# A recurrent attention block with a second network behind it: return transfers reordered, an inverse begun earlier in smaller portions, weight narrowing moved between engines

## The chip, the cores and the metric

The kernel runs on one core of a Trainium2 chip. The metric is the device time of one execution in microseconds (us), the median of several. Every kernel was timed in the same rounds and on the same chip as the kernel before, except the three leave-out kernels below, which ran once, with their profile; their state is unknown. The sets of rounds ran on different chips. A ratio is the mean time of one kernel's fast runs over that of the other's of the same rounds, so it is not quite the ratio of the medians quoted beside it; the bracket behind it is a 95% interval.

Engines: PE is TensorE (matmuls), PEld its weight loads, DVE is VectorE, ACT is ScalarE, POOL is GpSimd, SP is SyncE. `SPq` and `ACTq` are the DMA issues of SyncE and ScalarE.

## The reference

```python
# batch 4, 8 heads, 768 steps, head size 40; w in 0.85..0.95
for t in range(S):
    y[:, :, t] = einsum('bhd,bhde->bhe', r_t, state)
    Sa = einsum('bhde,bhe->bhd', state, a_t)
    state = state * w_t[..., None] - einsum('bhd,bhe->bhde', Sa, b_t) + einsum('bhd,bhe->bhde', v_t, k_t)
x = y as (3072, 320)
h = x @ w_in                                       # 320 x 1024
e = exp(h - max(h)); solu = h * e / (sum(e) + 1e-9)
out = ((solu - mean) / sqrt(var + 1e-6) * g_ln) @ w_out     # 1024 x 320
```

The kernel takes the 768 steps in 12 rounds of 64 steps, and each round in two "half-rounds", each with the 64 steps of 16 of the 32 pairs of batch and head: 24 half-rounds. Inside a round the dependence from step to step is a triangular system, so every round needs an inverse of 64 triangular 32x32 blocks. The weights of the second network come as float64 and are narrowed to float32 on the chip.

Of the kernel before, what the change touches and what calls it, by code (L numbers as in the profile page):

```python
# [52 lines left out]
def kernel(  # L53
# [101 lines left out]
    def narrow(dst, land, tmp):  # L155
# [9 lines left out]
        frac, rest = man.bitcast(FP32), low.bitcast(FP32)  # L165
# [3 lines left out]
        nc.scalar.activation(out=rest, in_=low.bitcast(U32), func=AF.Copy, scale=2.0 ** -52)  # L169
# [3 lines left out]
        yield  # L173
        nc.gpsimd.tensor_tensor(out=frac, in0=frac, in1=rest, op=ALU.add)
        nc.gpsimd.tensor_tensor(out=dst, in0=frac, in1=scale.bitcast(FP32), op=ALU.mult)
        yield

    def weights():
# [19 lines left out]
        if not exact:  # L198
            for tag in ("e", "lnT"):
                x = two.tile([P, 512], I64, tag=tag, name="bits", bufs=1)  # L200
                land += [x[:, 0:256], x[:, 256:512]]
            temps = [two.tile([P, 2, 256], I32, tag=tag, name="parts", bufs=1) for tag in ("osb", "parts")]
# [11 lines left out]
        for j in range(2):  # L214
            fetch(j)
        yield
        open_ = None
        for j, (dst, _) in enumerate(pieces):
            new = None if exact else narrow(dst, land[j % 4], temps[j % 2])
            for _ in range(2):  # L220
                for part in (open_, new):
                    if part:
                        next(part)
                if _:
                    fetch(j + 2)
                yield
            open_ = new
        for _ in range(2):
            if open_:
                next(open_)  # L230
# [3 lines left out]
        yield  # L234
# [3 lines left out]
        mean = bank("mean")  # L238
        for c in range(NF):
            nc.tensor.matmul(mean[:, 0:DM], lhsT=gb[:, c, :], rhs=w2[:, c, :], start=c == 0, stop=c == NF - 1)  # L240
        yield
        for c in range(NF):
            nc.vector.scalar_tensor_tensor(out=w2[:, c, :], in0=w2[:, c, :], scalar=g_col[:, c:c + 1],
                                           in1=mean[:, 0:DM], op0=ALU.mult, op1=ALU.subtract)
# [47 lines left out]
    def load(n, *names):  # L292
# [4 lines left out]
        for name in names:  # L297
# [7 lines left out]
            for c in range(2):  # L305
                nc.sync.dma_start(out=to[half(c)], in_=ap[2 * c:2 * c + 2, :, n * L:(n + 1) * L, :]
# [91 lines left out]
    def invert(n):  # L398
# [11 lines left out]
        for j in range(1, Q - 1):  # L410
# [6 lines left out]
            yield  # L417
        u_dram = of_round[n]["u"] = dram.tile([64, Q, Q], FP32, tag="u_dram", name="u_dram")
# [3 lines left out]
        for p in range(2):  # L422
            nc.sync.dma_start(out=u_dram.rearrange("b (c z) t -> b c z t", z=2)[:, :, p], in_=u[half(p)])
            if p == 0:
                nc.sync.dma_start(out=ut_dram, in_=ut)
        yield

    def bring_inverse(i):
# [5 lines left out]
        for q in (0, 2):  # L434
            for p in range(2):
                nc.sync.dma_start(out=tinv[quarter(q), :, p],
# [251 lines left out]
    def fronts(i):  # L688
# [3 lines left out]
    EARLY = ("r r a r W f r W W I r y W r W I a f a W s a f a W I W f s W I f a W L f",  # L692
             "r r a r W f g r W W I r y W r W I a f g a W s a f g a W I W f g s W I f g a W L f g")
    STEADY = "r b r a r f b b o r o I o r o y o r I o h a f L a s a h f a I h f s h f h a f h"
    front_of = {}

    front_of = {}

    front_of = {}

    front_of = {}

# [11 lines left out]
    def inverse_steps(i):  # L714

        if i < 3:
            return [[8, 8, 8, 8], [0, 3, 4, 3], [6, 6, 5, 5]][i]
        if i < LAG:
            return [0, 5, 5, 4] if i % 2 else [5, 5, 4, 4]
# [6 lines left out]
    with tc.manual_schedule():  # L726
        load(0, "w", "a", "b", "k")
        f, g = front(0), front(1)
        turns("f g", {}, f=f, g=g)
        load(1, "w", "a")  # L730
        turns("f g", {}, f=f, g=g)
        load(1, "b")
        turns("f f f f g g g g f g", {}, f=f, g=g)
        scatter(0)
        gather(0)
        load(0, "v", "r")
        load(1, "k")
        f, g, at, inv, so, ws = front(2), front(3), attend(0), invert(0), solve(0), weights()
        turns("f g f g f f g g", {}, f=f, g=g)
        load(2, "w", "a", "b", "k")  # L740
        turns("a a I a a W", dict(I=99), a=at, I=inv, W=ws)
        bring_inverse(0)
        turns("a f g a f g f g", {}, f=f, g=g, a=at)
        scatter(1)
        gather(1)
        load(1, "v", "r")
        begin(0)
        turns("s s", {}, s=so)
        inv = inverses()
        after, before = None, None  # L750
# [58 lines left out]
```

## The kernel before: what the change and the argument touch

One piece of weights is narrowed by operations spread over three engines (these are lines 162 to 175):

```python
    def narrow(dst, land, tmp):
        ...
        nc.vector.tensor_scalar(out=scale, in0=hi, ...)                  # L162
        nc.vector.tensor_scalar(out=man, in0=hi, ...)                    # L164
        yield
        nc.scalar.activation(out=scale, in_=scale, func=AF.Relu, ...)    # L167
        nc.scalar.activation(out=frac, in_=man, func=AF.Copy, ...)       # L168
        nc.scalar.activation(out=rest, in_=low.bitcast(U32), ...)        # L169
        yield
        nc.vector.scalar_tensor_tensor(out=scale, ...)                   # L171
        yield
        nc.gpsimd.tensor_tensor(out=frac, in0=frac, in1=rest, op=ALU.add)          # L174
        nc.gpsimd.tensor_tensor(out=dst, in0=frac, in1=scale..., op=ALU.mult)      # L175
        yield
```

The inverse is a chain of 30 steps on VectorE. Its blocks come through DRAM (`scatter`, then `gather` into `blk`), and its result goes back through DRAM (`u_dram`, `ut_dram`, then `tinv` and `tinvT`), because it is wanted with other rows on the partitions:

```python
    def invert(n):
        nc.vector.tensor_scalar(out=u[half(0)], in0=nb..., scalar1=-1.0, ...)      # u<-blk
        ...memsets...
        yield
        for j in range(1, Q - 1):                                                  # 30 steps
            nc.vector.tensor_tensor(out=t, in0=nb..., in1=u..., op=ALU.mult)       # prod<-blk,u
            nc.vector.tensor_tensor(out=u..., in0=u..., in1=t, op=ALU.subtract)    # u<-u,prod
            yield
        nc.vector.tensor_copy(out=ut, in_=...)                                     # ut<-u
        for p in range(2):
            nc.sync.dma_start(out=u_dram..., in_=u[half(p)])
            if p == 0:
                nc.sync.dma_start(out=ut_dram, in_=ut)
        yield
```

Every `yield` ends a portion. A string says in which order the portions of all parts are issued in a half-round, and with it the order of each engine's own instructions. `r` is the recurrence, `y` the read-out, `a` the next scores, `s` the use of the inverse (matmuls py and pz), `f` and `g` the decays of later half-rounds, `W` the narrowing, `I` the inverse:

```python
    EARLY = ("r r a r W f r W W I r y W r W I a f a W s a f a W I W f s W I f a W L f", ...)
    def inverse_steps(i):
        if i < 3:
            return [[8, 8, 8, 8], [0, 3, 4, 3], [6, 6, 5, 5]][i]
        ...
        for i in range(N):
            if i % 2 and (i + 3) // 2 < NCH:
                gather((i + 3) // 2)
            ...
            if more:
                bring_inverse(i + 1)               # tinv, tinvT on SyncE
            ...
            turns(EARLY[...] if i < LAG else STEADY, ...)        # LAG = 6
            if i % 2:
                load((i + 3) // 2, "v", "r")
                repack(i // 2)
            ...scatter
```

## Time and profile before

| | us |
|---|---|
| time, median of 3 runs | 729.5 (727.1 to 730.3) |
| first pu matmul (half-round 0 begins) | 56.6 |
| half-rounds 0 to 6, from pu to pu | 35.8, 34.0, 26.6, 31.7, 23.7, 36.3, 19.9: sum 208.0 |
| from there to the end | 463.4 |

"pu" is the first matmul of a half-round that needs the inverse, so the times between pu matmuls measure the half-rounds. From half-round 6 on the second network fills TensorE (busy 390.9 of the 405.3 us from 244.7 to 650). The granted clock in this trace is 0.5 or 1.0 in turn up to 244.9 us, 0.72 in the mean from 56.6 to 244.7, and 1.0 from there to 654.5. The views that the prediction rests on are in its text. One view that it did not use is the chain of work that ended last; this is its summary for 60 to 245 us, by line, as the answer gives it (cut at its right end):

```profile
by line: DVE prod L414 14.0%; DVE u L416 10.9%; issue 8.3%; DMA raw_b<-in_b_dram 5.7%; SPq L306 3.4%; PE mean L240 3.3%; DVE parts L162 2.9%; DVE parts L171 2.8%; PE pcx L341 2.4%; DVE parts L164 2.3%; DMA bits<-in_moe_w_out_dram 2.2%; DMA 
```

The two operations of the inverse (L414, L416) hold 24.9% of these 185 us, 46 us; VectorE's three narrowing operations (L162, L164, L171) hold another 8%.

### The profile page before, as it was taken

The page shows a single profiled execution, that of the slowest core. Times are in us where ns is not written, and L with a number is a line of the kernel's source. Part 1 is how long each engine was busy: PE and PEld are TensorE (multiplying, and loading weights), DVE is VectorE, ACT ScalarE, POOL GpSimd, SP SyncE. Part 2 cuts the span into 40 slices and gives each one's busy share as a digit, 9 for nine tenths or more (in the row PEclk, how much of TensorE's full clock was granted, in tenths as well). Part 3 has the DMA queues.
Part 4 walks back from the last instruction along what each step waited for, and adds up shares of the span by engine and source line. Part 5 has one row for each costly group of instructions (what it writes and reads, how often), then busy time and mean ns, then how long its engine had stood idle before and what let it go on. Part 6 is the DMA issues. An engine that isn't in the chain of part 4 may idle for free.

```text
span 728.0 us, 25509 instructions
## 1 busy us (share of the span) xinstructions
PE 605.3 (83%) x10873; PEld 431.6 (59%) x10873; DVE 467.5 (64%) x1258; ACT 267.2 (37%) x631; POOL 128.5 (18%) x228
## 2 busy tenths in 40 slices
PE   6436636665766899999999999999999899979997
PEld 4325525554554766677667676767677666645554
DVE  3565945855854678868868688696786763233442
ACT  4114333443441344343524443345334343322322
POOL 4104131332330111220212111220111000000000
PEclk9657576775876799999999999999999999998999
DMA  8946374455444443563555546536315231000001
GB/s 143 160 81 113 72 163 84 83 117 111 92 93 98 67 97 72 103 120 69 100 98 91 101 79 114 102 62 131 71 31 104 53 60 34 21 24 18 19 5 32
DMA packets 269793, 59.84 MB, mean 82 GB/s; under 512 B 255464, under 2 KB 265328, under 8 KB 269680
## 3 DMA queue, kind: packets, MB, share of 16 engines
q1 hardware_dynamic: 265680, 52.73, 39.8%
q10 hardware_dynamic: 4000, 5.48, 2.9%
q8 instruction: 86, 1.41, 0.8%
q14 instruction: 27, 0.22, 0.1%
HBM read 40.08 MB, written 13.37 MB: 73 GB/s over the span
## 4 chain that ended last, share of the span: by engine, by line
PE 58%; DVE 22%; DMA 7%; issue 5%; ACT 4%; SPq 3%; POOL 1%; ACTq 0%; DVEq 0%; POOLq 0%
PE po L662 14%; PE h L617 12%; DVE prod L414 7%; DVE u L416 6%; PE pyo L589 4%; PE plnT L657 3%; PE pcx L341 2%; PE pcum L328 2%; DVE nmax L627 2%; PE plamv L280 2%; PE py L484 2%; DMA raw_b<-in_b_dram 2%; PE pyo L511 2%; PE pvT L261 2%; PE ppsi L280 1%
## 5 line engine op out<-in xcount | busy, mean ns | idle before, releaser
L617 PE MATMUL h<-w_in,xT 128*128 128x512 f32 (+1 forms) x288 | 128.2, 635 | 3.9 <-DVE e L634 3.9
L662 PE MATMUL po<-w,lnT 128*128 128x320 f32 x384 | 114.8, 438 | 0.0
L414 DVE TENSOR_TENSOR prod<-blk,u 128x30 f32<-128x30 f32 (+4 forms) x360 | 107.0, 297 | 11.8 <-DMA blk<-blk_dram 1.0
L416 DVE TENSOR_TENSOR u<-u,prod 128x30 f32<-128x30 f32 (+4 forms) x360 | 101.5, 282 | 12.4
L662 PEld LDWEIGHTS po<-w,lnT 128*128 128x128 f32 x384 | 68.8, 190 | 26.2 <-issue 2.9
L331 POOL TENSOR_TENSOR kx<-raw_b,inv 128x320 f32<-128x320 f32 x24 | 20.7, 866 | 254.8 <-ACT inv L329 210.1
L627 DVE TENSOR_REDUCE nmax<-h 128x1 f32<-128x1024 f32 x24 | 29.3, 1221 | 44.8 <-PE h L617 44.8
L617 PEld LDWEIGHTS h<-w_in,xT 128*128 128x128 f32 (+1 forms) x288 | 38.2, 191 | 31.6 <-issue 29.7
L484 PE MATMUL py<-tinv,nt 32*32 32x32 f32 x768 | 20.6, 202 | 34.2 <-DMA tinv<-ut_dram 34.2
L667 ACT ACTIVATE osb<-po,rs 128x320 f32<-128x320 f32 x24 | 12.7, 527 | 97.2 <-PE po L662 86.4
L596 DVE TENSOR_TENSOR x<-pyo,kx 128x512 f32<-128x512 f32 x24 | 16.6, 690 | 45.2 <-PE pyo L589 44.5
L282 DVE TENSOR_TENSOR lamv<-plamv,cst 128x512 f32<-128x512 f32 x24 | 16.5, 689 | 39.8 <-PE plamv L280 39.8
L649 POOL TENSOR_TENSOR rs<-c,mhalf 128x1 f32<-128x1 f32 x24 | 13.2, 548 | 158.4 <-DVE c L648 158.4
L658 ACT COPY lnT<-plnT 128x512 f32<-128x512 f32 x48 | 27.6, 586 | 33.8 <-PE plnT L657 33.5
L631 ACT ACTIVATE e<-h,nmax 128x1024 f32<-128x1024 f32 x24 | 26.7, 1114 | 36.1 <-DVE nmax L627 36.1
L484 PEld LDWEIGHTS py<-tinv,nt 32*32 32x32 f32 x768 | 17.2, 112 | 36.7 <-issue 29.3
L634 DVE TENSOR_TENSOR e<-h,e 128x1024 f32<-128x1024 f32 x24 | 29.4, 1225 | 14.6 <-ACT e L631 14.2
L499 ACT ACTIVATE tinvT<-pz 32x256 f32<-32x256 f32 x48 | 17.9, 372 | 56.9 <-PE pz L484 56.6
L341 PEld LDWEIGHTS pcx<-cst,lw 128*128 128x128 f32 x192 | 29.1, 209 | 14.9 <-ACT y_mid L496 8.5
L341 PE MATMUL pcx<-cst,lw 128*128 128x132 f32 x192 | 33.6, 307 | 5.3 <-ACT y_mid L496 3.4
L657 PE MATMUL plnT<-cst,e 128*128 128x128 f32 x192 | 29.9, 285 | 5.7 <-DVE e L634 5.4
L575 POOL TENSOR_TENSOR sm<-tot,fac 128x320 f32<-128x320 f32 x20 | 14.8, 742 | 95.2 <-DVE tot L574 79.2
(104 smaller groups left out, 1121.3 us busy)
## 6 DMA issues: line engine op xcount, KB each, us to landing
blk<-blk_dram SPq DMA_DIRECT2D x24, 256.0 KB
raw_w<-in_w_dram SPq DMA_DIRECT2D x24, 160.0 KB
raw_a<-in_a_dram SPq DMA_DIRECT2D x24, 160.0 KB
raw_b<-in_b_dram SPq DMA_DIRECT2D x24, 160.0 KB
raw_k<-in_k_dram SPq DMA_DIRECT2D x24, 160.0 KB
v<-in_v_dram SPq DMA_DIRECT2D x24, 160.0 KB
r<-in_r_dram SPq DMA_DIRECT2D x24, 160.0 KB
out_dram<-osb SPq DMA_DIRECT2D x24, 160.0 KB
```

The lines of the kernel that those rows point to most:

```text
L341: nc.tensor.matmul(t[:, g * 132:g * 132 + 132], lhsT=pair(lw, 2 * j + g), rhs=cst[:, lo:lo + 132], start=True, stop=True)
L414: nc.vector.tensor_tensor(out=t, in0=nb[:, j:j + 1, j + 1:Q].to_broadcast([P, rows, m]), in1=u[:, 0:rows, j:j + 1].to_broadcast([P, rows, ...
L416: nc.vector.tensor_tensor(out=u[:, 0:rows, j + 1:Q], in0=u[:, 0:rows, j + 1:Q], in1=t, op=ALU.subtract)
L484: nc.tensor.matmul(t[quarter(out), c:c + Q], lhsT=lhs(p, g), rhs=rhs(p, g), start=True, stop=True)
L589: nc.tensor.matmul(t[half(p), c, g * W:g * W + used], lhsT=kb[half(c), j, 2 * g + p, :], rhs=lam[half(c), h % 2, h // 2, 0:used], start=i ...
L617: nc.tensor.matmul(h[:, j * 512:j * 512 + 512], lhsT=of_round[i // 2]["xT"][rows, kt, i % 2 * P:i % 2 * P + P], rhs=w_in[rows, 4 if kt == ...
L627: nc.vector.tensor_reduce(out=nmax, in_=h, axis=AX.X, op=ALU.max, negate=True)
L631: nc.scalar.activation(out=e, in_=h, func=AF.Exp, bias=nmax, accum_out=esum)
L634: nc.vector.tensor_tensor(out=q, in0=h, in1=e, op=ALU.mult)
L657: nc.tensor.transpose(out=t[:, j * P:(j + 1) * P], in_=q[:, f * P:(f + 1) * P], identity=ident)
L658: nc.scalar.copy(out=lnT[:, fs.start:fs.stop].rearrange("p f t -> p (f t)"), in_=t)
L662: nc.tensor.matmul(o[:, 0:DM], lhsT=lnT[:, f, :], rhs=w2[:, f, :], start=f == 0, stop=f == NF - 1)
```

## The change

Its intent: TensorE waited for inverted blocks that were issued behind bulk loads, so issue them first; begin the second inverse while the first one's result travels; cut the inverse into small portions so that nothing waits long behind it; take the narrowing's last two operations off GpSimd, beside which VectorE's operations took longer (an inverse step's product of 126 columns 0.85 us at 79.99, with GpSimd's narrowing running, and 0.29 us at 75.07, with GpSimd idle); and do the centring of `w2` in half-rounds 6 and 7, not in a burst before them. The diff, cut to its core:

```diff
@@ narrow
-        nc.scalar.activation(out=rest, in_=low.bitcast(U32), func=AF.Copy, scale=2.0 ** -52)
-        nc.gpsimd.tensor_tensor(out=frac, in0=frac, in1=rest, op=ALU.add)
-        nc.gpsimd.tensor_tensor(out=dst, in0=frac, in1=scale.bitcast(FP32), op=ALU.mult)
+        nc.vector.scalar_tensor_tensor(out=frac, in0=low.bitcast(U32), scalar=2.0 ** -52, in1=frac, ...)
+        nc.vector.tensor_tensor(out=dst, in0=frac, in1=scale.bitcast(FP32), op=ALU.mult)
@@ weights: three pieces fetched ahead instead of two; four sets of temporaries instead of two;
@@          the centring becomes a part of its own, centre()
@@ invert
+        other = nc.scalar if n == 0 else nc.sync
-                nc.sync.dma_start(out=ut_dram, in_=ut)
+                other.dma_start(out=ut_dram, in_=ut)
@@ bring_inverse: for i == 0, half of tinv is issued by ScalarE
@@ order of portions
-    EARLY = ("r r a r W f r W W I r y W r W I a f a W s a f a W I W f s W I f a W L f", ...
+    EARLY = ("r r a I r f r W r I W y I r W W a f L a I W s W a f a W I f s W I f a W I W f", ...
-        if i < 3:
-            return [[8, 8, 8, 8], [0, 3, 4, 3], [6, 6, 5, 5]][i]
+        if i == 0:
+            return [3, 3, 3, 3, 3, 3, 2]
         if i < LAG:
-            return [0, 5, 5, 4] if i % 2 else [5, 5, 4, 4]
+            return [0, 0, 2, 4, 4, 4, 3 if i < LAG - 1 else 0] if i % 2 else [3, 3, 3, 3, 3, 0, 0]
@@ start
-        load(0, "w", "a", "b", "k")
+        load(0, "w", by=(nc.sync, nc.scalar)); load(0, "a"); load(0, "b", by=act); load(0, "k")
+        load(0, "v", "r", by=act)                   # act: both halves issued by ScalarE
...
         scatter(0)
+        load(1, "k")
         gather(0)
+        load(2, "w", "a"); load(1, "v", "r")
-        turns("a a I a a W", dict(I=99), a=at, I=inv, W=ws)
-        bring_inverse(0)
+        turns("a f g W a a W f f W a g g W a", {}, f=f, g=g, a=at, W=ws)
+        turns("I f g f g I f g", dict(I=[8, 8]), f=f, g=g, I=inv)
+        scatter(1); load(2, "b", "k"); gather(1)
+        turns("I a", dict(I=99), a=at, I=inv)
+        bring_inverse(0)
...
+        turns("I s s", dict(I=12), s=so, I=inv)     # 12 portions of the second inverse
@@ main loop
+            if more and (i % 2 or i == 0):
+                bring_inverse(i + 1)                # ahead of the gather
             if i % 2 and (i + 3) // 2 < NCH:
                 gather((i + 3) // 2)
-                bring_inverse(i + 1)
...
             if i % 2:
+                if i + 2 < N:
+                    bring_inverse(i + 2)            # ahead of v, r, the repacking and the scatter
                 load((i + 3) // 2, "v", "r")
```

## The prediction

> **What bounds the kernel now.** I read the page first (clock and busy rows), then the busy table cut at four points, then the waits of one stage, then SyncE's, TensorE's and VectorE's instructions in order of time. A half-round is one value of the loop's index i; I mark it by the start of its matmul group pu: 56.6, 92.4, 126.5, 153.1, 184.8, 208.5, 244.7 and 264.6 us for i = 0 to 7. From i = 6 on, the second network's h and po matmuls fill TensorE.
>
> The busy table (columns: stretch, length, busy us of PE, PEld, DVE, ACT, POOL, granted clock, DMA share, GB/s) cut there:
>
> ```profile
> 0.00:56.60 56.60, 27.36 (x376) 21.37 (x376) 29.31 (x89) 14.43 (x31) 13.58 (x31) 0.73 0.77 127
> 56.60:244.70 188.10, 117.99 (x2500) 96.19 (x2499) 122.41 (x358) 71.22 (x191) 53.83 (x88) 0.72 0.52 100
> 244.70:650.00 405.30, 390.94 (x7757) 274.80 (x7757) 285.78 (x755) 161.85 (x374) 57.29 (x102) 1.00 0.42 79
> 650.00:728.00 78.00, 68.99 (x243) 39.22 (x241) 29.96 (x56) 19.72 (x35) 3.84 (x7) 0.94 0.08 20
> ```
>
> From 244.7 us TensorE is busy 96% of the time at full clock; that part cannot move much. Before it nothing is full: TensorE 63%, VectorE 65%, clock 0.72. So the gain has to come out of the first 245 us, where chains of waits rule. The waits of 56 to 245 us (total, times, longest):
>
> ```profile
> PE py L484 <- DMA tinv<-ut_dram: 32.5, 8, 12.8
> POOL w_in L175 <- DVE parts L171: 28.5, 5, 10.1
> DVE u L404 <- DMA blk<-blk_dram: 8.9, 3, 5.4
> DVE parts L162 <- POOL w_in L175: 7.6, 2, 7.0
> DVE parts L162 <- POOL w L175: 5.3, 2, 4.9
> ```
>
> TensorE waits 32.5 us for inverted blocks. VectorE waits 12.9 us for GpSimd's narrowing. Why the blocks are late shows on SyncE's queue:
>
> ```profile
> 93.07 2.38 SPq L306 DMA_DIRECT2D raw_b<-in_b_dram  x2
> 95.55 3.62 SPq L306 DMA_DIRECT2D raw_k<-in_k_dram  x2
> 99.26 2.74 SPq L389 DMA_DIRECT2D blk_dram<-nt  x4
> 103.49 1.12 SPq L396 DMA_DIRECT2D blk<-blk_dram  x2
> 109.32 1.79 SPq L436 DMA_DIRECT2D tinv<-ut_dram  x4
> ```
>
> ```profile
> 91.14 0.63 DVE L420 COPY ut<-u 128x512 f32<-128x512 f32 x1
> ```
>
> ```profile
> 111.89 0.28 PE L484 MATMUL py<-tinv,nt 32*32 32x32 f32 x2 [12.80 <-DMA tinv<-ut_dram]
> ```
>
> The second inverse is finished at 91.1 us, but its way back (tinv) is issued only at 109.3, behind b, k, the scatter and the next gather; TensorE idles 12.8 us.
>
> [...]VectorE in order of time, one step with GpSimd's narrowing beside it and the next without:
>
> ```profile
> 79.99 0.85 DVE L414 TENSOR_TENSOR prod<-blk,u 128x126 f32<-128x126 f32 x1
> 80.87 0.29 DVE L416 TENSOR_TENSOR u<-u,prod 128x126 f32<-128x126 f32 x1
> ```
>
> [...]the DMA engines' busy share is already 0.85 to 1.17 from 2 to 16 us. [...]
>
> **The change part by part.**
>
> *Narrowing.* 26 pieces (10 of 256 columns, 16 of 160) lose two GpSimd operations and one ScalarE operation each, and gain two on VectorE. [...]the existing scalar_tensor_tensor (L171, same sizes) starts its successor after 0.33 or 0.24. So VectorE gains 10 x 0.66 + 16 x 0.48 = 14.3 us. It gets back contention: the 60 big instructions of an inverse take 16.4 us busy between 220 and 262 us (no narrowing) but 18.8, 19.7 and 19.1 in the three before, 8.4 us together, and the 12.9 us waits on GpSimd go. So about neutral in VectorE's time, better in coupling.
>
> *Inverted blocks first.* From i = 1 the order on SyncE is u, ut, u, scatter, tinv and tinvT, then gather, then the odd half's blocks, v, r, xT. Way back instead of 18 us from the end of the inverse to the issue: u's issues 2, scatter 3, landing about 4.5 in parallel, tinv issue, landing: first py about 9.5 us after ut, as in the undisturbed first inverse (44.5 us end, 52.6 most of py). That removes the 12.8 and the 8.7 us waits of i = 1 and i = 3, and most of those of even i.
>
> *First inverse.* Against it: v, r and three weight pieces (0.65 and 0.79 MB) are now issued before the first scatter. At the 165 GB/s seen there this is over 8 us of transfers in a stretch that is already full, of which I put 7 ahead of or beside scatter and gather; ScalarE spends about 3.4 us issuing loads in the front chain, inside this. The first inverse (24.2 us now) starts near 31, carries two kx and two nt (2.7 us) inside, loses some contention, ends near 53.5. Its return with two issuing queues takes about 11 us to pu instead of 12: first pu near 64.6, **8 us later** than now. In that return VectorE starts the second inverse (u must first be read out, some 4 us; then 1.4 + 11 steps at 0.5), so 14 of its 31 portions are done when lamu of i = 0 comes.
>
> *Half-rounds.* VectorE's work in one, read from distances of starts: half an inverse 9.5 (30 steps 17.1, set-up 1.4, ut 0.6), five narrowed pieces at 1.4 or 1.0, masks and sums 6 x 0.6 + 2 x 0.4 = 4.4. TensorE's: about 13.5 us at full clock, up to 20 at half.
> - 0 to 1: pu to lamu 4.5, then 17 steps 9.7, five pieces 7, other 4.0, ut and nt 1.2, hand-over 1: 27 (now 35.8).
> - 1 to 2: 2.2 + 9.8 + 6.6 + 4.4 + 1 = 24 on VectorE; TensorE: py 8.2 after pu, then 14.6 as now, 23. So 24 (now 34.1).
> - 2 to 3, 3 to 4, 4 to 5: 2 + 9.5 + 5.1 + 4.4 + 1.5, so 22.5, 23, 22 (now 26.6, 31.7, 23.7).
> - 5 to 6: the centring (mean: 3.9 us wait and 6.1 us at half clock) is gone from here, narrowing too; TensorE sets it: 20 (now 36.2).
> - 6 to 7: 19.9 plus the mean matmuls at full clock, 3.1, and about 1 of waiting for gb: 24 (now 19.9).
>
> Sum 162.5 against 208.0: 45.5 saved, minus 8 at the start: **37.5**. After i = 7 nothing changes, since TensorE is the bound there and its work is the same. 729.5 - 37.5 = **692 us**.
>
> **Rivals.**
> *VectorE becomes the bound of the early stage and takes the gain.* For it: by my sums it is 85 to 90% full in i = 1 to 4, [...]and ScalarE's narrowing waits for it (43.7 us of such waits now), so a late VectorE delays copies that TensorE needs. If each of i = 1 to 4 costs 4 us more: 708. Against: the inverse comes in portions of two to four steps, so chain work waits at most about 2 us.
> *The early loads cost more than they give.* [...]the first scatter may stand behind all the weight bytes. Start 15 us later rather than 8: 699. If instead the small transfers slip through, 4 us: 688.
> *The clock helps more than I count.* If the early stage runs at full clock, the TensorE-led pieces of i = 1 to 5 shrink by 2 to 3 us each: about 680. [...]
> *The gain is hidden*, the second network's work catching up at the end. Against: from 244.7 us on TensorE has no idle time to absorb it, so an earlier begin of i = 6 is an earlier end.
>
> **Range and chances.** The rivals give 680 to 708; the sum has seven terms of 1.5 to 4 us error each and a start of 4: 677 to 709 should hold it 8 times in 10. Slower than 715 needs the first two rivals together and more: faster by over 2% 0.92, within 2% 0.07, slower 0.01.
>
> **What would show it.** First u step near 31 us, first pu near 64.6; second inverse's ut near 90; pu of i = 6 near 203 and of i = 7 near 227, and equal distances from there to the end. PE py waits on tinv after 70 us under 8 us in total. Inverse instructions near 17 us each with no 0.7 us ones beside narrowing. VectorE over 80% busy from 65 to 183 us. The prediction is wrong if the first pu comes after 72 us, if the half-rounds of i = 1 to 4 stay above 26 us, or if a new wait (TensorE for ScalarE copies behind narrowing) exceeds 15 us.

## The result, and the profile after

The changed kernel takes **737.7 us** (735.0 to 740.7, 4 runs) against 728.7 (727.1 to 730.3, 4 runs) for the kernel before in the same rounds: ratio 1.012 [1.008, 1.017]. It is not faster, it is 1% slower. Behind the narrowing and its helpers, line numbers of the changed kernel are 5 to 6 higher than before. The profiled run of the changed kernel took 740.7 us, the slowest of its four; that of the kernel before took 729.8 us.

| us | before | predicted | after |
|---|---|---|---|
| first inverse starts | 24.2 | 31 | 35.1 |
| first pu | 56.6 | 64.6 | 70.3 |
| half-round 0 | 35.8 | 27 | 30.5 |
| 1 | 34.0 | 24 | 34.5 |
| 2 | 26.6 | 22.5 | 26.8 |
| 3 | 31.7 | 23 | 33.7 |
| 4 | 23.7 | 22 | 26.4 |
| 5 | 36.3 | 20 | 24.2 |
| 6 | 19.9 | 24 | 26.7 |
| sum of these | 208.0 | 162.5 | 202.8 |
| from there to the end | 463.4 | unchanged | 465.8 |

Predicted were +8 at the start and -45.5 in the half-rounds; the profiled run has +13.7, -5.2, and +2.4 in the rest, together +10.9. So two terms failed: the half-rounds by 40 us, the start by 6.

The busy table of the changed kernel, cut at its own first pu and sixth half-round (columns as in the prediction):

```profile
0.00:70.30 70.30, 24.47 (x378) 19.55 (x378) 33.45 (x113) 15.68 (x35) 13.47 (x31) 0.74 0.78 131
70.30:246.40 176.10, 116.98 (x2483) 96.39 (x2482) 119.13 (x379) 61.43 (x159) 22.27 (x36) 0.69 0.47 94
```

VectorE is busy 119 of 176 us, 68% against 65% before: still not full. The granted clock was 0.69, against 0.72. The waits of 70 to 246 us (total, times, longest):

```profile
ACT parts L167 <- DVE parts L162: 51.5, 15, 11.2
PE py L490 <- ACT vT L268: 20.1, 3, 10.5
DVE u L409 <- DMA blk<-blk_dram: 16.3, 3, 6.1
PE py L490 <- DMA v<-in_v_dram: 10.4, 1, 10.4
```

TensorE's wait for tinv, 32.5 us before, is gone. In its place py waits 30.5 us for something else: 20.1 for ScalarE's copy vT and 10.4 put down to v. What that is shows in half-round 1. First SyncE, then VectorE, ScalarE and TensorE of the changed kernel in order of time:

```profile
104.84 3.21 SPq L442 DMA_DIRECT2D tinv<-ut_dram  x4
108.15 1.89 SPq L445 DMA_DIRECT2D tinvT<-u_dram  x4
110.08 1.13 SPq L401 DMA_DIRECT2D blk<-blk_dram  x2
```

```profile
106.95 0.68 DVE L602 TENSOR_TENSOR x<-pyo,kx 128x512 f32<-128x512 f32 x1
113.72 0.42 DVE L409 TENSOR_SCALAR u<-blk 64x512 f32<-64x512 f32 x1 [6.10 <-DMA blk<-blk_dram]
...
117.05 0.28 DVE L162 TENSOR_SCALAR parts<-bits 128x256 int32<-128x256 int32 x1
```

```profile
117.37 0.51 ACT L167 ACTIVATE parts<-parts,ebias 128x256 int32<-128x256 int32 x1 [9.70 <-DVE parts L162]
117.58 0.35 ACTq L211 DMA_DIRECT2D bits<-in_moe_w_out_dram  x1
117.79 0.40 ACT L168 ACTIVATE parts<-parts 128x256 f32<-128x256 int32 x1
118.09 0.56 ACT L268 COPY vT<-pvT 128x512 f32<-128x512 f32 x1
```

```profile
118.71 1.13 PE L490 MATMUL py<-tinv,nt 32*32 32x32 f32 x32 [10.37 <-DMA v<-in_v_dram]
```

Read from the bottom: py begins at 118.71. tinv was issued at 104.84, so it is not the cause any more. py starts 0.06 us after the end of the copy vT (118.09, 0.56 us long). py does not use vT; but the program gives py the PSUM bank that the copy reads out, and the waits above hold 20.1 us of py for this copy. vT stands in ScalarE's order behind the narrowing L167, which waited 9.70 us for VectorE's L162. L162 stands in VectorE's order behind the head of the next inverse, `u<-blk`, and that waited 6.10 us for `blk`, whose gather is now issued behind tinv and tinvT. VectorE, ScalarE and TensorE stand in a convoy, one behind the other, and at its head is one transfer. The waits stand behind one another in the order in which the program issues the portions: 6.10 us on VectorE, 9.70 on ScalarE and 10.37 on TensorE.

At the start, ScalarE's first issues and its first activation:

```profile
4.91 3.50 ACTq L311 DMA_DIRECT2D v<-in_v_dram  x2
8.46 3.98 ACTq L311 DMA_DIRECT2D r<-in_r_dram  x2
12.49 0.83 ACT L329 ACTIVATE lw<-raw_w 128x320 f32<-128x320 f32 x2 [10.47 <-DMA raw_k<-in_k_dram]
```

Before, this activation began at 5.86. ScalarE is held 7.5 us issuing v and r (four issues of 1.05 to 2.12 us, and 1.2 us of wait between two of them), and its first arithmetic stands behind that.

### The profile page after: what moved, and what is told of

It is laid out like the page before. It is cut to its first block, busy times and chain, and to the rows that moved or that the text cites.

```text
span 738.9 us, 25449 instructions
## 1 busy us (share of the span) xinstructions
PE 609.6 (83%) x10873; PEld 436.0 (59%) x10873; DVE 471.5 (64%) x1310; ACT 260.4 (35%) x606; POOL 97.7 (13%) x176
## 4 chain that ended last, share of the span: by engine, by line
PE 59%; DVE 23%; DMA 6%; ACT 5%; issue 4%; SPq 2%; ACTq 1%; DVEq 0%
PE po L668 14%; PE h L623 12%; DVE prod L419 6%; DVE u L421 6%; PE pyo L595 4%; PE plnT L663 3%; DMA blk<-blk_dram 3%; PE pcum L333 2%; PE plamv L285 2%; PE pcx L346 2%; DVE nmax L633 2%; PE pyo L517 2%; PE py L490 2%; PE plamu L285 2%; ACT e L637 1%
## 5 line engine op out<-in xcount | busy, mean ns | idle before, releaser
L421 DVE TENSOR_TENSOR u<-u,prod 128x30 f32<-128x30 f32 (+4 forms) x360 | 97.8, 272 | 12.4
L419 DVE TENSOR_TENSOR prod<-blk,u 128x30 f32<-128x30 f32 (+4 forms) x360 | 96.3, 267 | 10.5
L336 POOL TENSOR_TENSOR kx<-raw_b,inv 128x320 f32<-128x320 f32 x24 | 20.8, 866 | 312.1 <-ACT inv L334 287.0
L490 PE MATMUL py<-tinv,nt 32*32 32x32 f32 x768 | 19.9, 204 | 47.8 <-ACT vT L268 20.1
L633 DVE TENSOR_REDUCE nmax<-h 128x1 f32<-128x1024 f32 x24 | 29.3, 1220 | 43.5 <-PE h L623 43.5
L623 PEld LDWEIGHTS h<-w_in,xT 128*128 128x128 f32 (+1 forms) x288 | 37.7, 189 | 30.9 <-issue 28.9
L602 DVE TENSOR_TENSOR x<-pyo,kx 128x512 f32<-128x512 f32 x24 | 16.6, 690 | 50.4 <-PE pyo L595 50.0
L505 ACT ACTIVATE tinvT<-pz 32x256 f32<-32x256 f32 x48 | 17.9, 373 | 64.3 <-PE pz L490 61.7
L637 ACT ACTIVATE e<-h,nmax 128x1024 f32<-128x1024 f32 x24 | 26.7, 1114 | 36.7 <-DVE nmax L633 36.7
L640 DVE TENSOR_TENSOR e<-h,e 128x1024 f32<-128x1024 f32 x24 | 29.4, 1224 | 14.4 <-ACT e L637 13.9
L346 PE MATMUL pcx<-cst,lw 128*128 128x132 f32 x192 | 33.2, 302 | 6.3 <-ACT rT L268 3.9
L287 DVE TENSOR_TENSOR lamv<-plamv,cst 128x512 f32<-128x512 f32 x24 | 16.6, 690 | 30.3 <-PE plamv L285 30.3
L333 PE MATMUL pcum<-lw,cst 128*128 128x320 f32 x48 | 22.7, 564 | 15.3 <-ACT lw L329 13.5
L663 PE MATMUL plnT<-cst,e 128*128 128x128 f32 x192 | 30.5, 289 | 5.6 <-DVE e L640 5.3
```

The costliest lines, as they stand in the source:

```text
L333: nc.tensor.matmul(t[:, 0:DM], lhsT=c_("cum_in"), rhs=lw[:, :, 0:D], start=True, stop=True)
L346: nc.tensor.matmul(t[:, g * 132:g * 132 + 132], lhsT=pair(lw, 2 * j + g), rhs=cst[:, lo:lo + 132], start=True, stop=True)
L419: nc.vector.tensor_tensor(out=t, in0=nb[:, j:j + 1, j + 1:Q].to_broadcast([P, rows, m]), in1=u[:, 0:rows, j:j + 1].to_broadcast([P, rows, ...
L421: nc.vector.tensor_tensor(out=u[:, 0:rows, j + 1:Q], in0=u[:, 0:rows, j + 1:Q], in1=t, op=ALU.subtract)
L490: nc.tensor.matmul(t[quarter(out), c:c + Q], lhsT=lhs(p, g), rhs=rhs(p, g), start=True, stop=True)
L623: nc.tensor.matmul(h[:, j * 512:j * 512 + 512], lhsT=of_round[i // 2]["xT"][rows, kt, i % 2 * P:i % 2 * P + P], rhs=w_in[rows, 4 if kt == ...
```

## The experiments

Seventeen kernels besides the changed one ran on the chip. Their diffs are cut to the core, that of the lag is condensed; marks like `...` stand for what is left out. "Gather first", below, is the changed kernel with one exchange (the second experiment), and later experiments build on it. All results agree with the reference, except where said.

| kernel | median us (range) | ratio to before |
|---|---|---|
| changed kernel | 737.7 (735.0–740.7) | 1.012 [1.008, 1.017] |
| changed, first loads from SyncE | 737.6 (733.9–741.1) | 1.011 [1.007, 1.015] |
| changed, gather first | 723.5 (721.6–724.6) | 0.991 [0.989, 0.994] |
| changed, inverse begun late | 725.5 (724.4–726.4) | 0.994 [0.992, 0.996] |
| changed, narrowing back on GpSimd | 729.4 (728.2–732.2) | 1.001 [0.998, 1.004] |
| gather first and late | 729.4 (725.9–732.8) | 0.997 [0.993, 1.001] |
| changed, all first loads from SyncE | 734.5 (732.1–734.8) | 1.003 [1.001, 1.006] |
| changed, gather behind first return | 736.9 (735.2–738.3) | 1.007 [1.004, 1.010] |
| before, late centring alone | 728.9 (726.3–730.3) | 0.996 [0.993, 0.999] |
| gather first, old start | 725.2 (723.3–726.9) | 0.993 [0.989, 0.997] |
| gather first, no inverse steps | 691.4 (one run) | |
| gather first, no narrowing | 700.6 (one run) | |
| gather first, lag | 719.2 (717.0–723.4) | 0.986 [0.982, 0.990] |
| gather first, old start, return from SyncE | 722.1 (718.8–724.0) | 0.988 [0.984, 0.992] |
| the same, lag | **717.5** (716.2–718.3) | **0.982** [0.979, 0.986] |
| before, inverted blocks first alone | 729.8 (728.8–730.3) | 0.999 [0.996, 1.002] |
| before, no inverse steps | 684.4 (one run) | |
| the 717.5 version, weights behind the return | 723.8 (722.2–726.5) | 0.992 [0.990, 0.994] |

The kernel before was at 729.5 to 731.2 us in these rounds.

### Is the convoy the cause? Gather first; inverse late

Two ways to keep VectorE from standing at the head of the next inverse. One puts the gather back ahead of the inverted blocks:

```diff
-            if more and (i % 2 or i == 0):
-                bring_inverse(i + 1)
             if i % 2 and (i + 3) // 2 < NCH:
                 gather((i + 3) // 2)
+            if more and (i % 2 or i == 0):
+                bring_inverse(i + 1)
```

> The changed kernel with the order of before on SyncE: the gather of the next round's blocks ahead of the inverted blocks of this one. Theory C (in the changed kernel VectorE stands 6.1 us at i = 1 and 3 before the first portion of the next inverse, waiting for its gather, and the narrowing's ScalarE part and the copies behind it stand too, so py waits 10 us): VectorE's waits for blk shrink under 2 us each, py waits for tinv itself again, half-rounds 1 and 3 change by less than 3 us in sum, total within 4 us of 738. Rival O (inverted blocks first is a pure gain that other parts of the change hide): half-rounds 1 and 3 longer by 6 us or more each, total 748 or more. Rival O' (the new order is the harm): total 728 or less.

The other leaves the order of transfers and begins the next inverse later in odd half-rounds:

```diff
-            return [0, 0, 2, 4, 4, 4, 3 if i < LAG - 1 else 0] if i % 2 else [...]
+            return [0, 0, 0, 0, 5, 6, 6 if i < LAG - 1 else 3] if i % 2 else [...]
```

> The changed kernel with the portions of the inverse in odd half-rounds moved behind py: 0 0 0 0 5 6 6 instead of 0 0 2 4 4 4 3, so that no inverse step that needs the gathered blocks stands in VectorE's order before the work that py waits for. Theory C (VectorE stands in order before the gathered blocks and takes ScalarE and TensorE with it): VectorE's waits for blk in half-rounds 1, 3 and 5 under 1 us, the wait before py in half-round 1 down from 10.4 to about 3 us, half-rounds 1, 3 and 5 shorter by 4 to 6 us each at first and up to 2 given back where the portions are now larger: total 725 to 730. Theory V (VectorE is simply full with the narrowing it took over): VectorE's idle time moves but half-rounds stay within 1.5 us, total within 3 us of 738.

Measured: 723.5 and 725.5, so each takes back what the change lost, and they are 6.5 and 4.4 us below the kernel before of these rounds. The late inverse came out in the range that theory C gave. The gather first did not: theory C had expected a total within 4 us of 738 and half-rounds 1 and 3 shorter by less than 3 us in sum (6.0 measured); the total is that of rival O', that the new order is the harm. SyncE shows why: the gather came 3.7 us earlier (106.38 instead of 110.08 us) and tinv only 2.8 us later (107.61 instead of 104.84), so both were early enough. Its waits, to be set beside those of the changed kernel (16.3 us for blk; 30.5 us of py for vT and v):

```profile
PE py L490 <- ACT vT L268: 25.0, 4, 8.1
...
DVE u L409 <- DMA blk<-blk_dram: 5.3, 2, 3.2
```

So the convoy is real, and on SyncE the changed order does harm; but most of py's wait stays when blk comes in time, and what holds vT then is examined below. The half-rounds 1 to 5 became 31.3, 24.7, 30.9, 25.6, 21.1 with the gather first, and 29.8, 27.0, 29.6, 26.0, 20.8 with the late inverse. They did not fall to the predicted 20 to 24. TensorE's waits with the late inverse, 71 to 245 us:

```profile
PE py L490 <- ACT vT L268: 15.3, 4, 5.3
PE pu L556 <- DVE x L537: 14.5, 3, 5.3
```

VectorE no longer waits for blk, but now pu waits 14.5 us for VectorE's sum x, which stands behind the portions of the inverse that were moved later. The wait moved once more.

Both at once:

> The changed kernel with both cures of the convoy at once: the gather of the next inverse ahead of the inverted blocks on SyncE, and the next inverse begun late in odd half-rounds. Theory C (one convoy: VectorE stands at the head of the next inverse, whose blocks have not landed, and ScalarE's narrowing and copies and TensorE stand behind it): both cure the same wait, so the two do not add: 719 to 724 us against 723.5 and 725.5 apart. Rival, two separate costs (blocks late; VectorE full early in the half-round): they add, about 711 us.

It gave 729.4, worse than either. Half-rounds 1 and 3 are 31.3 and 29.7, no better than with one of them, so these two cure one wait and do not add, as the theory said; but half-round 5 lengthened to 24.2 and the later half-rounds by 2 us, which neither expectation has (both gave less than 725), and which was not followed up. (Its profile is of a run of 731.6 us, 2 us above its median.)

### Narrowing back on GpSimd

```diff
-        nc.vector.scalar_tensor_tensor(out=frac, in0=low.bitcast(U32), scalar=2.0 ** -52, in1=frac, ...)
-        nc.vector.tensor_tensor(out=dst, in0=frac, in1=scale.bitcast(FP32), op=ALU.mult)
+        nc.gpsimd.tensor_tensor(out=frac, in0=frac, in1=rest, op=ALU.add)
+        nc.gpsimd.tensor_tensor(out=dst, in0=frac, in1=scale.bitcast(FP32), op=ALU.mult)
```

(and ScalarE's operation for `rest` back)

> The changed kernel with the narrowing's addition and product back on GpSimd (and the third ScalarE operation), all else as changed. Theory V (the 14 us that VectorE took over are what ate the gain): half-rounds 1 to 4 shorter by about 2.5 us each, total 727 to 730. Theory C: the stand before blk is the same, contention with GpSimd comes back (about 2.5 us an inverse), half-rounds unchanged or longer: total 737 to 744.

729.4, 8 us below the changed kernel: the total that theory V gave. Half-rounds 1 to 4 (33.2, 25.2, 33.1, 25.1) fell by only 1.2 us each on average, not 2.5, and VectorE's wait for blk stayed (16.0 us). So taking the narrowing off GpSimd removes contention (the inverse's two operations sum to 194.1 us in the changed kernel, against 208.5 before and 205.2 here), but costs more than it gives back. That the cost lies in VectorE's order is argued, not shown. The narrowing on GpSimd together with the gather first was not run.

### What VectorE's work costs: leave it out

These three tell the most. First the 30 steps of every inverse after the first are left out, on "gather first"; set-up, read-out and all transfers stay. This is not the reference's arithmetic and no version to keep, although its result still passed the comparison.

```diff
         for j in range(1, Q - 1):
+            if n > 0:
+                yield
+                continue
```

> The version with the gather first, but of every inverse after the first only the set-up, the read-out and the transfers are left: its 30 steps on VectorE are gone, so the result is wrong on purpose. Theory V (TensorE waits in the early half-rounds because its scores, sums and copies stand in VectorE's order behind portions of the inverse, directly and through ScalarE): half-rounds 1 to 4 fall from 31.3, 24.7, 30.9, 25.6 us to 21 to 24 each, and the waits of py and pu fall under 8 us together. Rival (a chain through TensorE and ScalarE sets the half-round whatever VectorE does): they stay above 25 us on average.

Then the narrowing, its seven operations replaced by one copy on GpSimd (wrong result):

> The version with the gather first, with the narrowing's five VectorE and two ScalarE operations a piece replaced by one copy on GpSimd: wrong result on purpose, same transfers. Theory V expects half of what leaving out the inverse gives, since it is 5 to 7 us of VectorE in a half-round against 9: half-rounds 1 to 4 shorter by 3 us each on average, py waiting for the copy vT under 8 us in all instead of 25. Rival (only the inverse's portions block, the narrowing slips into gaps): under 1 us each.

And the first cut on the kernel before:

> The kernel before without the 30 steps of each inverse after the first (its set-up, read-out and transfers stay; not the reference's arithmetic). Theory V (VectorE's time for the inverse is paid in full in the early stage, before and after the change): about 30 us below the kernel before, near 698, as in the changed order (32 below). Rival (before, TensorE waited for transfers, so VectorE's time was hidden there, and the change only exposed it): less than 15 us below.

| four half-rounds, 1 to 4 | time us | VectorE busy us | TensorE busy us | granted clock |
|---|---|---|---|---|
| before | 116.0 | 76.8 | 71.2 | 0.72 |
| before, no inverse steps | 93.5 | 41.4 | 64.3 | 0.80 |
| gather first | 112.5 | 78.4 | 74.5 | 0.70 |
| gather first, no inverse steps | 97.0 | 50.4 | 67.6 | 0.77 |
| gather first, no narrowing | 98.5 | 54.1 | 72.1 | 0.76 |

The first two rows are read from these lines:

```profile
92.42:208.45 116.03, 71.17 (x1656) 59.03 (x1656) 76.83 (x224) 47.63 (x133) 37.44 (x63) 0.72 0.52 102
83.09:176.63 93.54, 64.33 (x1658) 53.38 (x1657) 41.37 (x105) 47.26 (x133) 36.97 (x60) 0.80 0.63 128
```

A microsecond of VectorE's work left out takes 0.63 us off the time in the kernel before (22.5 for 35.4), 0.56 and 0.58 with the gather first. These figures hold more than VectorE's order: the granted clock rose too, by 0.06 to 0.08, and TensorE's busy time fell by 2.3 to 6.9 us for the same matmuls; and without the narrowing ScalarE's work fell as well (41.9 to 29.8 us). How much of the gain each of these gives was not separated. Half-rounds 1 to 4 of "gather first" become 26.1, 22.3, 23.9, 24.6 without the inverse: the first and the last of them missed the expected 21 to 24, and py still waited 16.7 us for vT, so the waits did not fall under 8 as theory V expected; the times fell all the same. Without the narrowing, py's wait for vT fell to 9.8 (under 8 expected), and the four half-rounds became 3.5 us shorter on average (3 expected).

On the kernel before, the run without the inverse is the sharpest. Its waits between 56 and 245 us:

```profile
PE py L487 <- DMA tinv<-ut_dram: 30.6, 8, 12.6
```

TensorE still waits 30.6 us for tinv, nearly as much as before (32.5), with nearly the same longest wait. Yet the kernel takes 684.4 us, 45 less than the 729.5 on the same chip, where theory V expected 30. About 37 of the 45 us are won before half-round 7 begins (at 227.7 instead of 264.6 us), the rest behind it. The chain that ended last, by engine, in the kernel before and in this one:

```profile
PE 58%; DVE 22%; DMA 7%; issue 5%; ACT 4%; SPq 3%; POOL 1%; ACTq 0%; DVEq 0%; POOLq 0%
```

```profile
PE 72%; DMA 9%; DVE 7%; SPq 4%; ACT 3%; issue 3%; POOL 1%; DVEq 0%; POOLq 0%; ACTq 0%
```

VectorE falls from 22% of 728 us (160) to 7% of 683 (48); most of that share goes to TensorE, so the chain's share is not the time to be won. But in the early half-rounds of both orders more than half of the inverse's time on VectorE is paid for, although VectorE is busy only 65% of the time, and this gain does not need the wait to go that the change set out to remove.

### Inverted blocks first, alone, on the kernel before

```diff
+            if more and (i % 2 or i == 0):
+                bring_inverse(i + 1)
             if i % 2 and (i + 3) // 2 < NCH:
                 gather((i + 3) // 2)
...
-                bring_inverse(i + 1)
...
             if i % 2:
+                if i + 2 < N:
+                    bring_inverse(i + 2)
                 load((i + 3) // 2, "v", "r")
```

> The kernel before with one part of the change alone: inverted blocks issued ahead of the gather, and the odd half-round's ahead of v, r, the repacking and the scatter. The prediction's step: the waits of py for tinv, 32.5 us in all, nearly go and about 20 us of time with them: 710. Rival (the wait is exchanged: the next inverse's blocks come later, VectorE stands at their head, and ScalarE's narrowing and TensorE behind it): waits of py for tinv under 10 us, VectorE's for blk up by more than 10, and the total within 5 us of the kernel before.

729.8 against 729.5: nothing, with 0.999 [0.996, 1.002]. Its waits of 56 to 245 us, to be set beside those that the prediction shows:

```profile
DVE u L404 <- DMA blk<-blk_dram: 24.9, 3, 8.7
...
PE py L484 <- DMA tinv<-ut_dram: 9.6, 4, 5.2
```

py's wait for tinv falls by 22.9 us (32.5 to 9.6), VectorE's for blk rises by 16.0 (8.9 to 24.9), and the half-rounds (33.8, 27.3, 32.6, 24.8 for 1 to 4) are those of before within 1.2 us. py also gets waits for ScalarE that it did not have before, 5.8 us for vT and 4.6 for an operation of the narrowing. The rival holds in all its numbers. This step by itself is worth zero, because the wait is exchanged; the prediction had counted most on it. What the wait would be worth if nothing else came later, no run shows.

### ScalarE's part one portion later ("lag")

```diff
             for turn in range(2):
-                if open_ and turn == 0:
-                    next(open_)
-                if new:
+                if new and turn == 0:
                     next(new)
+                if open_:
+                    next(open_)
                 if turn:
                     fetch(j + 3)
                 yield
             open_ = new
```

> The version with the gather first, with ScalarE's part of every narrowed piece issued one portion later, so that VectorE's first part lies further back. Theory (ScalarE stands behind a VectorE operation that itself stands behind the inverse, and the copy vT behind ScalarE): py's waits for vT fall from 25 to under 12 us, total 2 to 6 us below 723.5. Rival (the later portion also stands behind a portion of the inverse; the wait only moves): within 2 us of 723.5.

719.2: 4 us below "gather first", in the expected range; py's waits for vT fell to 12.2 us, just over the expected 12 (in a profiled run of 723.4 us, the slowest of the four). ScalarE's wait for L162 (43.5 us with the gather first) fell to 3.1, with 8.9 for another of VectorE's narrowing operations: so what coupled the two engines was in good part that ScalarE was given work that VectorE had not yet come to.

### The start

Five kernels, because each showed another cause.

*First loads as before, v and r behind the first gather.*

```diff
-        load(0, "w", by=(nc.sync, nc.scalar)) ... load(0, "v", "r", by=act)
+        load(0, "w", "a", "b", "k")
...
         gather(0)
+        load(0, "v", "r")
```

> The changed kernel with the first loads as before: all of w, a, b, k from SyncE, and v and r of round 0 from SyncE behind the first gather; the weight pieces stay early on ScalarE. Theory S (ScalarE is held by issuing v and r [...]3.5 and 4.0 us in the trace of the changed kernel, so its first Ln starts at 12.5 instead of 5.9 us): first Ln near 6 us, first step of the first inverse near 28 instead of 35 us, first pu near 64 instead of 70.3, total 6 to 7 us faster than the changed kernel, 731. Rival (the early transfers as such fill the DMA engines, whoever issues them; v and r only come later now and the weights still stand before the scatter): first inverse no earlier than 33 us, total within 2 us of 738.

737.6, no gain. The first activation is back at 5.8 us, but the first inverse starts at 38.1: the changed order puts the scores that need v and r ahead of the inverse on VectorE, and with v and r late they hold it (the copy vT of these scores runs at 31.53 us, in the changed kernel at 25.9). The rival's numbers came true (no earlier than 33 us, total within 2 us of 738), but the run mixed two things up and decides nothing.

*All first loads from SyncE, v and r with them:* `load(0, "w", "a", "b", "k", "v", "r")`.

> The changed kernel with every first load, v and r among them, on SyncE in the order w, a, b, k, v, r. Theory S (ScalarE's first activations are late only because it was held while issuing v and r; the first inverse is late because of that): the first decay starts near 6 us instead of 12.5, the first inverse near 29 instead of 35.1, the first pu near 65 instead of 70.3, total 5 to 6 us below the changed kernel, about 732. Rival (the first inverse is late because the forward steps of the first scores are put ahead of it on VectorE, whatever the loads): the first inverse stays above 33 us and the total above 735.

734.5: first activation at 5.9, but the first inverse at 33.8, not 29, and the first pu at 68.9, 1.4 us earlier. At the first pu ScalarE's hold is worth 1.4 us; the rest is neither theory's:

```profile
20.89 3.46 SPq L394 DMA_DIRECT2D blk_dram<-nt  x4
24.45 1.78 SPq L311 DMA_DIRECT2D raw_k<-in_k_dram  x2
30.26 1.12 SPq L401 DMA_DIRECT2D blk<-blk_dram  x2
```

The blocks were written by VectorE at 18.8 us, scattered from 20.9, and gathered only at 30.3, 9.4 us after the scatter's issue; before it was 4.4 (16.30 to 20.71 us). Between them stands the load of k that the change puts there (1.78 us), and SyncE waits for weight pieces to land, 2.6 us at the gather. The prediction's rival "the early loads cost more than they give" is this.

*Gather of the second inverse behind the first one's return* (one line, `gather(1)`, moved behind `bring_inverse(0)`).

> The changed kernel with the gather for the second inverse issued behind the first inverse's return instead of ahead of it. Theory (that gather waits on SyncE for the read-out of ut, and u's read-out stands behind it): the way from the end of the first inverse to the first pu falls from 14.4 to about 11.5 us, but the second inverse's blocks land later; total 1 to 3 us below the changed kernel. Rival (the return is bound by the transfers themselves): the first pu is within 1 us of 70.3 and the total is the same.

First pu 67.6, 2.7 us earlier, as the theory said; but the second inverse waits 11.9 us for its blocks, half-round 0 grows from 30.5 to 34.2, and the total is 736.9. The 95% interval of the ratio (1.004 to 1.010) overlaps that of the changed kernel. A gain at one place, given back at the next.

*The old start,* on "gather first": loads and order from before up to the first pu, and `[5, 5, 5, 5, 4, 4, 4]` portions of the second inverse in half-round 0. Two things stay as changed: half of the return is issued by ScalarE, and four more portions of the narrowing stand beside it.

> The version with the gather first (723.5 us) and, besides, the kernel before's order from the first load to the first pu: no weights, v or r ahead of the first scatter, the first inverse ahead of the forward steps of the scores, the second inverse begun only in half-round 0. Theory (the new start costs 14 us at the first pu and gives back 5 in half-round 0): first pu near 57 us, half-round 0 near 35, all later half-rounds as with the gather first, total near 714. Rival (the second inverse, not begun early, and the narrowed pieces, fewer by then, come due later and take it back): the later half-rounds grow and the total is 720 or more.

725.2, a total in the rival's range, but not for the rival's reason. The first inverse starts at 25.0 and ends at 44.8 as before, but the first pu comes at 64.5. SyncE's longest wait between 28 and 60 us:

```profile
SPq L311 <- DMA ut_dram<-ut: 13.9, 1, 13.9
```

L311 is a load of b for a later round. It shares no data with ut. What the traces of the kernel before and of the changed one show of this: the 646 issues of both queues carry eight semaphore numbers between them, 80 or 81 issues to each. In all 638 pairs of successive issues with one number, the landing records of the first end before the second is issued; in 17 of these pairs before and 28 in the changed kernel the second follows the last record within 0.2 us (there SyncE's blk, which shares no data with ut either, waited 5.7 us and was issued at 58.66 us, 0.06 us after ScalarE's ut had landed). In the run here the second half of b, on SyncE, was held in the same way until ScalarE's ut had landed: the first half was issued at 32.63 us, the second at 47.46. u, tinv and tinvT stood behind it. With these transfers on SyncE again:

```diff
-        other = nc.scalar if n == 0 else nc.sync
+        other = nc.sync
...
-                (nc.scalar if i == 0 and q else nc.sync).dma_start(out=tinv[...
+                nc.sync.dma_start(out=tinv[...
```

> The last version with the kernel before's start (gather first besides), and now the first inverse's way back issued wholly from SyncE, as before, instead of half from ScalarE. Theory (in the run with the old start the first pu came at 64.5 instead of 57 us because a load of b on SyncE stood 13.9 us for ScalarE's ut transfer, with which it shares no data, and u, tinv and tinvT behind it): that wait is gone, first pu near 57.5, total 717 to 721. Rival (the narrowing put beside the return costs the 7 us): first pu stays above 62 and the total at 725.

722.1, the first pu at 61.2: half of the expected way. The wait of 13.9 us is gone, but another of 9.6 us, for a weight piece, stands in its place. With the lag besides:

> The same, with ScalarE's part of each narrowed piece one portion later: all that helped so far in one kernel. If the gains add (start 5, lag 4 on 723.5), about 714, 2.2% below the kernel before. Rival (they relieve the same wait): 718 or more.

**717.5 us**, 1.8% below the kernel before and 2.7% below the changed one (737.7, in other rounds), the best of all. Of the steps from "gather first" (0.991) to here only the whole is clear of noise; the intervals of neighbouring steps overlap. The gains add only in part: first pu 61.6, half-rounds 36.2, 30.2, 25.4, 30.5, 24.2, 19.7, 25.4. Its longest wait on SyncE between 40 and 60 us is, again, one on weights:

```profile
SPq L446 <- DMA bits<-in_moe_w_in_dram: 7.6, 2, 7.4
```

So the last kernel fetches the first weights only behind the first inverse's return:

> The best version so far with the first weight pieces fetched and narrowed only behind the first inverse's way back. In its trace tinv's issue stood 7.4 us for the landing of a weight piece. Theory: that wait is gone, the first pu near 57 instead of 61.6 us, and 3 to 5 us of it stay in the total: 713 to 715. Rival (the pieces, five portions later, come due in the early half-rounds or in a burst before half-round 6): total within 1.5 us of 717.5.

A miss: 723.8, first pu 63.0. Now the return's second transfer, ut, waited 5.5 us for g_rows, a small load of the second network. The source has g_rows behind the return, and ScalarE issued it only at 49.32 us, 4.6 us after the first part of u (44.72); yet ut, issued at 50.81, stood behind its landing. In this run who waited for whom followed neither the source nor the time. The kernel before's own arrangement, one portion of weights ahead of the return and none beside it (first pu 56.6), was not run with the gather first.

### The late centring alone

The kernel before with `centre()` as in the change, from half-round 6 on.

> The kernel before with the late centring alone. If the traces' gaps are to be added (36.3 to 24.2 us in one half-round, 19.9 to 26.7 in the next), it is 5 us faster, about 724. Rival (the next half-round gives it all back): within 2 us of the kernel before.

728.9 against 731.2: 0.996 [0.993, 0.999], some 3 us. It lies between the expected 5 and the rival's 2. The gain of half-round 5 (36.3 to 28.2) is partly given back in 6 (19.9 to 25.4).

## Why the prediction was wrong

**The bound.** Right: nothing is full in the early stage, chains rule it, and after half-round 7 nothing changes (465.8 against 463.4 us). Wrong: "chains of waits" were sized by the waits' totals. TensorE's 32.5 us for tinv were taken for time to be won. The runs show otherwise from both sides: taking 22.9 us of this wait away changed nothing, since other waits came in its place, and taking VectorE's steps away while 30.6 us of it remained gave 45 us. The chain of work that ended last pointed at the inverse (46 us of it in 60 to 245 us; that the two numbers are so close is chance). The prediction did not use it.

**Inverted blocks first.** The mechanism of the way back was right: tinv is issued 5.9 us after ut in the changed kernel (98.9 to 104.8), 18.2 before, and the wait for it is gone. (The 9.5 us from ut to py that the prediction reads from the first inverse are 8.1 in the times it names, 44.5 to 52.6; nothing hangs on this.) The failed step is "That removes the 12.8 and the 8.7 us waits of i = 1 and i = 3": it was checked what the moved transfers overtake, but not what then waits for the overtaken ones. The overtaken gather stands at the head of VectorE's next inverse.

**The half-rounds**, 162.5 predicted, 202.8 measured. This is the term that was wrong by 40 us. Most of them were worked out as VectorE's work laid end to end plus about 1 us. The work itself was sized rightly: in half-rounds 1 to 4 VectorE was busy 78.5 us, 86% of the predicted 91.5, as "85 to 90% full" has it. The step that failed is the end to end: these half-rounds took 121.4 us, and VectorE was idle in 43 of them. From 65 to 183 us it was busy 69%, where the prediction named over 80% as its sign (68% before). It does not get its work end to end: it takes turns with TensorE and ScalarE in a fixed order, and leaving work out between the turns shortened them by 0.56 to 0.63 us for each us, the faster clock included. (Without the inverse's steps the seven half-rounds of "gather first" come to 162.8 us. That this is the predicted sum is chance: the prediction counts about 9.5 us of the inverse in most of them.)

**"The inverse comes in portions of two to four steps, so chain work waits at most about 2 us."** This set aside the rival that came true in part, that VectorE takes the gain: VectorE was not full, but ScalarE's narrowing waited for it, as the rival says (51.5 us, 43.7 before). A portion's length bounds the wait only if the portion can run when it is reached. The first one could not (6.1 us for blk in half-round 1), and the wait went on to ScalarE (9.70) and TensorE (10.37). Two of the three signs of failure that the prediction named came: half-rounds 1 to 4 above 26 us (34.5, 26.8, 33.7, 26.4), and TensorE behind ScalarE's copies behind the narrowing for over 15 us (30.5). The third, a first pu after 72 us, did not (70.3).

**Narrowing, "about neutral in VectorE's time, better in coupling".** The first half was right: VectorE's busy time over the whole kernel went from 467.5 to 471.5 us, and the contention that the move removes was seen rightly (the inverse's two operations 194.1 us instead of 208.5). The second was not: in the changed order the move costs 8 us (737.7 against 729.4 with the operations back on GpSimd).

**The first inverse**, "8 us later": 13.7. Its own length was right (20.8 us with the added work inside; 22.5 predicted). Too small were the loads ahead of it (start at 35.1, not 31), where ScalarE's hold (6.6 us at the first activation, 1.4 of it in the time) and the gather behind bulk and weights (9.4 us instead of 4.4 in the run that separates them) come together, and the return, 14.4 us instead of the predicted 11.

**The centring.** Half-round 5 gave 12.1 us of the predicted 16; half-round 6 took 6.8 and not 4. Its mean matmuls, 6.1 us before, ran at a granted clock of 0.5 up to 221.0 us, half of that time, and at 1.0 from there; in the changed kernel, at 1.0, they took 4.6 us, not 3.1. Alone it is worth 3 us. The mechanism was right; the sizes of what is won and given back were not.

**The rest.** The 2 to 3 us that the rival "the clock helps more than I count" has for each of i = 1 to 5 at full clock are the author's estimate; the clock came out lower (0.69 against 0.72). What stays open: what moves the granted clock between 0.5 and 1.0, which no run shows; how much of what the leave-out runs gave is VectorE's order and how much the clock; whether the narrowing on GpSimd adds to the gather first; why "gather first" and "late inverse" together are slower than either, and what holds the first pu at 61.6 us in the best version beyond the wait for weights.

## What to carry to other kernels

A wait in the profile is worth its length only if what it waits for can come earlier without something else coming later, and if the waiting engine's chain is the one that ends last; so read the chain of work first, and leave the suspected work out once in a wrong-result run before reordering around it. Here 22.9 us less of one wait gave 0 us, as others took its place, and 35 us less of VectorE's work gave 22.5 in four half-rounds. VectorE was 65% busy, with its instructions alternating with others in a fixed order, and work on it was still paid for at 0.56 to 0.63 of its length. When transfers are reordered, list what is overtaken and who stands in order behind it; and before you issue a transfer from a second queue, look in the trace whether both queues take their semaphores from one small set: here it was eight numbers for 646 issues, and one load stood 13.9 us for a transfer of the other queue with which it shares no data.
